# Second-layer rows of a two-layer mixture of experts: whole rows turned by TensorE, or quarter rows turned by VectorE in 32 by 32 squares

## The chip, the cores and the metric

One core of one Trainium2 chip runs the whole program. The metric is the device time of one execution in microseconds (us). Before the change it is 563.17 us, the median of three runs (561.17 to 566.2).

## What is computed

An attention without softmax, an RMS norm, and two layers of a mixture of experts with one expert per token. Cut to what matters here, the second layer:

```python
N, D, E, F = (2304, 512, 8, 1024)
expert_idx = np.argmax(x @ w_gate, axis=1)
gate_w = probs[np.arange(N), expert_idx]
...
disp[e, counts[e]] = x[i]          # rows sorted by expert
h = np.maximum(np.einsum('ecd,edf->ecf', disp, w1), 0.0)
y = np.einsum('ecf,efd->ecd', h, w2)
out[i] = gate_w[i] * y[expert_idx[i], pos[i]]
```

All tensors are float32. The first layer is the same, on the normed output of the attention.

## The kernel before

**Blocks.** Each layer is a list of blocks: a block holds up to 320 rows of one expert. The second layer has ten, counted from 0 here; their widths are 256, 256, 256, 268, 320, 260, 176, 160, 144 and 256 rows, for the experts in places 0, 0, 1, 1, 2, 3, 4, 5, 6 and 7 of an order by load. The function moe() runs them one after the other. Phase 1 of a block multiplies w1 with the block's rows (tiles hps on TensorE, eight steps `fc`), phase 2 multiplies w2 with what phase 1 gave (tiles acc, eight steps again). A product of two float32 numbers is made of three matmuls of rounded parts (h for high, l for low: lines 1275, 1276, 1277), and in blocks 6 to 8, under 192 rows wide ("plain"), of one float32 product (line 1273). The weights come as eight pieces per expert through SP's queue (raw, or w where a block is plain); ScalarE makes the high part of a piece (line 1169), VectorE the low part (line 1172).

**How rows reach a block.** The first layer stores its result by rows in DRAM (x2d). While block k runs, GpSimd gathers the rows of block k+1 into tiles xg of up to 128 rows: one indirect DMA per tile (line 1201), four xg buffers. A tile has rows on the partitions and 512 values along them; the matmuls want it turned, values on the partitions. x_tile() does that with four TensorE transposes of 128 by 128 into PSUM (xps, line 1251). ScalarE then writes the high part xh (line 1259) and VectorE the low part xl (line 1267). These steps are taken up one by one in phase 2 of block k, one after each `fc` from 1 on; every engine works its own instructions in program order. In the same steps an odd `fc` takes one piece of the next expert's w1 (ScalarE's high part, VectorE's low part), if block k+1 has another expert and is not plain. The first matmuls of block k+1 read xh, and the second one xl, over the whole width of the block.

**The first layer has both ways.** From its fourth block on its rows are gathered in quarters: gather_quarters() issues one indirect DMA for 32 rows, 128 partitions of 128 values each (line 1212), and x_squares() turns a tile with one VectorE instruction on 32 by 32 squares (xw, line 1226). ScalarE and VectorE then read xw where they would have read xps.

**What else is on the queues.** GpSimd also scatters the results: blocks 3 to 8 in quarters (line 1460, one indirect DMA per 32 rows, after a VectorE product with the gate, line 1456), the other blocks in tiles of 128 rows (line 1326). All indirect DMAs stand in one queue, in program order. final() works out the routing of the layer in small VectorE steps; rest() is its last part, and by_quarter() copies three kinds of numbers to the partitions of the quarters by four small matmuls.

```python
for k, b in enumerate(blocks):
    ...
    if k and nb and (m or "gi" in rt):
        nb.gather()
    ...
        slot(fc % 2, ahead, RATES[m][1] if nb else THEN2)
        ...
        if fc:
            run(xs, 1)
```

Here nb is the next block, xs the list of its turning steps, and slot() takes the pieces of weights, the scatters and the routing steps.

Of the kernel before, what the change touches and what calls it, by code (L numbers as in the profile page):

```python
# [11 lines left out]
F32 = mybir.dt.float32  # L12
# [11 lines left out]
N, DM, E, F = 2304, 512, 8, 1024  # L24
# [7 lines left out]
DC = DM // 128  # L32
# [33 lines left out]
OFF = (1152, 1536)  # L66
# [27 lines left out]
def plain(c):  # L94
    return slice(128 * c, 128 * c + 128)
# [6 lines left out]
def up(w):  # L102
    return (w + 31) // 32 * 32
# [75 lines left out]
class Kernel:  # L179
# [546 lines left out]
    def rest(self, m, rt, lo, hv, ncol, nt, c0, x=""):  # L726

        V = self.nc.vector
        A = [128, nt, ncol]
        k = 2 + m  # L730
        got = rt["got"]
        parts = rt["parts"] + ([self.tokw[:, 0:ncol]] if m else [])
        pv = self.rp.tile([128, k, nt, ncol], F16, tag="pv" + x, name="pv" + x)
        for i in range(k):
            V.tensor_tensor(out=pv[:, i], in0=hv[:, 0], in1=bc(parts[i], 1, A), op=ALU.mult)
            yield 0.4
        yield 2 * PE_WAIT
        ps = yield from self.picked(lo, pv, ncol, nt, k)
        val = self.t([128, 2, nt], F32, "G" + x)
        G = val[:, 0]  # L740
        V.tensor_copy(out=G, in_=ps[:, 0])
        V.scalar_tensor_tensor(out=G, in0=ps[:, 1], scalar=1 / 4096, in1=G, op0=ALU.mult, op1=ALU.add)
        if m:
            none = self.t([128, nt], F32, "none" + x)
            V.tensor_scalar(
                out=none, in0=got[:, 0], scalar1=-4096.0, scalar2=float(4096 + OFF[0]), op0=ALU.mult, op1=ALU.add
            )
            si = self.t([128, nt], I32, "si" + x)
            V.tensor_tensor(out=si, in0=ps[:, 2], in1=none, op=ALU.add)
            rt["si"] = si  # L750
            V.tensor_tensor(out=val[:, 1], in0=ps[:, 2], in1=none, op=ALU.add)
        elif c0 is not None:
            V.tensor_copy(out=self.aux[:, c0:c0 + nt, E], in_=got[:, 1])
            V.tensor_copy(out=self.aux[:, c0:c0 + nt, E + 1], in_=got[:, 0])
        self.hold = False
        rt["G"] = G
        yield
        if rt is self.rt[1]:
            yield 2 * PE_WAIT
            ps = yield from self.by_quarter(val.rearrange("p k n -> p (k n)"), 2 * nt)  # L760
            G4 = rt["G4"] = self.t([128, nt, 4], F32, "ex")
            V.tensor_copy(out=G4, in_=ps[:, :, 0:nt].rearrange("p g n -> p n g"))
            rt["si4"] = self.quarter_rows(ps[:, :, nt:], 0, "gi4")
            self.hold = False
            yield

# [451 lines left out]
    def x_squares(self, m, xg, n, xh, xl, o):  # L1218

        nc = self.nc  # L1220
        k = up(n) // 32
        src = xg[:, 0:k, 0:128].rearrange("p g (c d) -> p c g d", c=4)
        xw = self.mp.tile([128, DC, 128], F32, tag="xw", name="xw", bufs=2)

        def turn():
            nc.vector.transpose(out=xw[:, :, 0:32 * k].rearrange("p c (g t) -> p c g t", t=32), in_=src)  # L1226

        return [turn, lambda: self.x_parts(m, xw[:, :, 0:n], xh, xl, o, n)]
# [16 lines left out]
    def x_tile(self, m, x, n, xh, xl, o, ps=None):  # L1245

        if ps is None:
            ps = self.pt.tile([128, 512], F32, tag="t", name="xps")
        ps = ps.rearrange("p (a b) -> p a b", a=4)
        for dc in range(DC):  # L1250
            self.nc.tensor.transpose(  # L1251
                out=ps[:, dc, 0:n], in_=x[:n, plain(dc)], identity=self.c("ident")[:n, :n]
            )
        self.x_parts(m, ps[:, :, 0:n], xh, xl, o, n)

# [518 lines left out]
    def run(self):  # L1774
# [10 lines left out]
        ]  # L1785
        for b in self.blocks[0][SQUARES:]:
            b.squares = True
        for b in self.blocks[1]:
            b.turned = b.w % 128 > 0
        self.feed = [Feed(self, m) for m in range(2)]  # L1790
        self.rp = ctx.enter_context(tc.tile_pool(name="route", bufs=1))
        self.rawp = ctx.enter_context(tc.tile_pool(name="raw", bufs=4))
# [21 lines left out]
class Block:  # L1814
# [15 lines left out]
    def gather(self):  # L1830
        if self.xgs or self.xt or self.squares and "gi4" not in self.rt:
            return
        for t in range(tiles_of(self.w)):
            n = min(128, self.w - 128 * t)
            self.xgs.append((
                self.k.gather_quarters(self.m, self.t0 + t, n) if self.squares else
                self.k.gather(self.m, self.rt["gi"], self.t0 + t, n, self.known), n,
            ))
        if self.squares:
            for xg, n in self.xgs:  # L1840
                self.k.normal(xg[:, 0:up(n) // 32], 128, self.k.nc.gpsimd)

# [110 lines left out]
def pieces(name, a):  # L1953

    if name == "moe2_w2":
        a = a.reshape(E, F, 4, DC, 32).transpose(0, 1, 3, 2, 4).reshape(E, F, DM)
    if name.endswith("w1"):
        return a.reshape(E, DC, 128, 4, 256).transpose(0, 3, 2, 1, 4).reshape(E, 4, 128, 1024)
    return a.reshape(E, 4, 2, 128, DM).transpose(0, 1, 3, 2, 4).reshape(E, 4, 128, 1024)
# [43 lines left out]
```

## Time and profile before

| | |
|---|---|
| median of three runs | 563.17 us (561.17 to 566.2) |
| the profiled execution | 565.43 us, of it 563.6 us in the span of its instructions |
| TensorE busy | 97% of the span, 3980 matmuls |
| VectorE, ScalarE, GpSimd busy | 56%, 41%, 32% |
| granted TensorE clock, mean | 0.992 of full speed |

The profile is one execution on the chip. An instruction's row names the engine, the line, what it writes and reads, and its duration; starts are in us from the first instruction. Matmuls overlap, so that a matmul's own duration (0.28 us, say) is longer than the step from one start to the next. The second layer's blocks 2 to 9 lie between some 354 and 558 us.

### The profile page before, as it was taken

To read this page: it belongs to the slowest core of one execution; us is meant where nothing else is said; L and a number is where in the kernel's file an instruction comes from. 1 tells how busy PE (TensorE), PEld (TensorE's weight loads), DVE (VectorE), ACT (ScalarE), POOL (GpSimd) and SP (SyncE) were. 2 spreads that over 40 slices of the span, in tenths; PEclk is the share of its full clock that TensorE was granted. 3 is DMA by queue.
4 is the path that set the end of the run, shared out by engine and by line. 5 is a ranking of instruction groups with operands and counts; after the bars stand their busy time and mean duration, and the time that the engine had idled before them with its cause. 6 is when DMAs were issued, how large, how long until landed. Compare 5 with 4: busy or idle time off the path is not lost.

```text
span 563.6 us, 10439 instructions
## 1 busy us (share of the span) xinstructions
PE 544.5 (97%) x3980; PEld 516.2 (92%) x3980; DVE 316.5 (56%) x742; ACT 231.4 (41%) x414; POOL 178.3 (32%) x182
## 2 busy tenths in 40 slices
PE   7899999999999999999989999999999999999995
PEld 6889769999999999999978988989899999999994
DVE  1357962677666667767787695375146562221470
ACT  0255422344555555555553541255243532211440
POOL 1232313475526070812001001212312725643241
PEclk9999999999999999999998998999999999999999
DMA  8996935256555565665545514246234656889531
GB/s 307 389 371 232 393 91 189 95 181 218 179 167 175 178 197 182 205 199 180 188 155 185 176 45 150 75 149 211 74 99 158 204 190 199 273 248 333 197 110 41
DMA packets 34229, 106.93 MB, mean 190 GB/s; under 512 B 6664, under 2 KB 6794, under 8 KB 34171
## 3 DMA queue, kind: packets, MB, share of 16 engines
q1 hardware_dynamic: 24432, 81.95, 42.9%
q0 software_dynamic: 7072, 19.48, 11.1%
q10 hardware_dynamic: 2667, 4.75, 2.5%
q8 instruction: 33, 0.54, 0.4%
q14 instruction: 25, 0.20, 0.1%
HBM read 91.83 MB, written 14.60 MB: 189 GB/s over the span
## 4 chain that ended last, share of the span: by engine, by line
PE 73%; DVE 8%; DMA 7%; issue 5%; POOL 4%; ACT 2%; SPq 0%; POOLq 0%; ACTq 0%; DVEq 0%
PE hps L1275 8%; PE hps L1276 8%; PE hps L1277 8%; PE acc L1275 7%; PE acc L1277 7%; PE acc L1276 7%; PE hps L1273 7%; PE acc L1273 6%; PE yps L1405 3%; POOL xg L1212 3%; DMA qkv<-in_v_dram 2%; PE o L406 2%; PE kv L1273 2%; PE xps L1251 2%; DMA qkv<-in_k_dram 2%
## 5 line engine op out<-in xcount | busy, mean ns | idle before, releaser
L1275 PE MATMUL hps<-xh,w1h 128*128 128x256 f32 (+9 forms) x448 | 132.4, 296 | 0.0
L1276 PE MATMUL hps<-xl,w1h 128*128 128x256 f32 (+9 forms) x448 | 130.2, 291 | 1.0 <-DVE xl L1263 0.9
L1277 PE MATMUL hps<-xh,w1l 128*128 128x256 f32 (+9 forms) x448 | 129.7, 289 | 0.0
L1296 ACT ACTIVATE hh<-hps 128x256 fp32r<-128x256 f32 (+13 forms) x144 | 54.6, 379 | 149.7 <-PE hps L1277 99.7
L1275 PE MATMUL acc<-hh,w2h 128*128 128x320 f32 (+8 forms) x320 | 95.6, 299 | 0.0
L1277 PE MATMUL acc<-hh,w2l 128*128 128x320 f32 (+8 forms) x320 | 94.4, 295 | 0.0
L1276 PE MATMUL acc<-hl,w2h 128*128 128x320 f32 (+8 forms) x320 | 94.4, 295 | 0.0
L1276 PEld LDWEIGHTS hps<-xl,w1h 128*128 128x128 f32 x448 | 84.8, 189 | 1.9 <-DVE xl L1263 1.5
L1275 PEld LDWEIGHTS hps<-xh,w1h 128*128 128x128 f32 x448 | 84.8, 189 | 1.6 <-issue 1.5
L1277 PEld LDWEIGHTS hps<-xh,w1l 128*128 128x128 f32 x448 | 84.8, 189 | 0.0
L1298 DVE SCALAR_TENSOR_TENSOR hl<-hps,hh 128x256 fp32r<-128x256 f32 (+9 forms) x112 | 49.0, 439 | 53.6 <-ACT hh L1296 53.2
L1212 POOL DMA_INDIRECT xg<-x1d,gi x54 | 55.0, 1019 | 72.9 <-DVE xw L1226 58.9
L1460 POOL DMA_INDIRECT out_dram<-y,gi x44 | 49.7, 1131 | 67.7 <-DVE y L1456 51.4
L1172 DVE TENSOR_TENSOR w2l<-raw,w2h 128x1024 fp32r<-128x1024 f32 x48 | 58.6, 1222 | 20.3 <-ACT w2h L1169 20.3
L1172 DVE TENSOR_TENSOR w1l<-raw,w1h 128x1024 fp32r<-128x1024 f32 x48 | 58.8, 1242 | 14.2 <-ACT w1h L1169 13.5
L1275 PEld LDWEIGHTS acc<-hh,w2h 128*128 128x128 f32 x320 | 61.1, 191 | 0.3
L1276 PEld LDWEIGHTS acc<-hl,w2h 128*128 128x128 f32 x320 | 61.2, 191 | 0.0
L1277 PEld LDWEIGHTS acc<-hh,w2l 128*128 128x128 f32 x320 | 61.1, 191 | 0.0
L1169 ACT ACTIVATE w2h<-raw 128x1024 fp32r<-128x1024 f32 x48 | 50.5, 1054 | 5.6 <-ACT y L1409 5.6
L1169 ACT ACTIVATE w1h<-raw 128x1024 fp32r<-128x1024 f32 x48 | 49.2, 1048 | 0.0
L1273 PE MATMUL acc<-hh,w 128*128 128x224 f32 (+3 forms) x256 | 40.9, 314 | 0.0
L1273 PE MATMUL hps<-xh,w 128*128 128x224 f32 (+3 forms) x256 | 39.4, 313 | 0.1
(308 smaller groups left out, 778.0 us busy)
## 6 DMA issues: line engine op xcount, KB each, us to landing
raw<-in_moe_w_dram SPq DMA_DIRECT2D x96, 512.0 KB, 3.4
w<-in_moe_w_dram SPq DMA_DIRECT2D x32, 512.0 KB, 4.7
x1d<-xs POOLq DMA_DIRECT2D x4, 1056.0 KB, 6.4
qkv<-in_k_dram SPq DMA_DIRECT2D x8, 512.0 KB, 9.0
qkv<-in_v_dram SPq DMA_DIRECT2D x8, 512.0 KB, 8.5
qkv<-in_q_dram SPq DMA_DIRECT2D x8, 512.0 KB, 7.3
x2d<-y ACTq DMA_DIRECT2D x15, 256.0 KB, 2.5
xg<-x1d,gi POOLq DMA_INDIRECT x57, 2.9
```

The lines of the kernel that those rows point to most:

```text
L406: T.matmul(out=ps[:, pair, 0:144], lhsT=qt[b, i // 2][:, at:at + 128], rhs=kvs[b][:, pair], start=True, stop=True)
L1169: self.nc.scalar.activation(out=h, in_=t, func=ACTF.Copy)
L1172: (self.nc.gpsimd if eng == "P" else self.nc.vector).tensor_tensor(out=l, in0=t, in1=h, op=ALU.subtract)
L1212: self.nc.gpsimd.indirect_dma_start(out=xg[:, g], out_offset=None, in_=(self.X1, self.X2)[m].rearrange("n (q x) -> (n q) x", q=4), in_offs ...
L1273: nc.tensor.matmul(out=out, lhsT=a[0], rhs=b[0], start=start, stop=stop)
L1275: nc.tensor.matmul(out=out, lhsT=a[0], rhs=b[0], start=start, stop=False)
L1276: nc.tensor.matmul(out=out, lhsT=a[0], rhs=b[1], start=False, stop=False)
L1277: nc.tensor.matmul(out=out, lhsT=a[1], rhs=b[0], start=False, stop=stop)
L1296: nc.scalar.activation(out=hh[:, fc, :], in_=ps, func=ACTF.Relu)
L1298: nc.vector.scalar_tensor_tensor(out=hl[:, fc, :], in0=ps, scalar=0.0, in1=hh[:, fc, :], op0=ALU.max, op1=ALU.subtract)
L1405: nc.tensor.matmul(out=ps[:n, j, :], lhsT=yt[:, dc, 128 * t:128 * t + n], rhs=self.iwg[:, dc, :], start=True, stop=True)
L1460: self.nc.gpsimd.indirect_dma_start(out=out, out_offset=bass.IndirectOffsetOnAxis(ap=rt["si4"][:, g - g0, t0 + t:t0 + t + 1].bitcast(U32), ...
```

## The change

Blocks 3 to 9 of the second layer take the way of the first layer's later blocks: rows gathered in quarters, turned by one VectorE instruction per tile. In the first layer a square holds 32 neighbouring values of a quarter row. Here the values stand in another order: chunk c of the turned tile takes every fourth value, so that VectorE reads its input with a step of four values (16 bytes). The rows of w1 of the second layer are put in the same order ahead of the run, and so blocks 0 to 2, still turned by TensorE, read every fourth column too (`x[:n, dc::DC]` as the operand that is loaded as weights). rest() works out one more table, the gather indices of the quarters.

```diff
-        val = self.t([128, 2, nt], F32, "G" + x)
+        val = self.t([128, 2 + m, nt], F32, "G" + x)
...
             V.tensor_tensor(out=val[:, 1], in0=ps[:, 2], in1=none, op=ALU.add)
+            V.tensor_copy(out=val[:, 2], in_=got[:, 1])
...
-            ps = yield from self.by_quarter(val.rearrange("p k n -> p (k n)"), 2 * nt)
+            ps = yield from self.by_quarter(val.rearrange("p k n -> p (k n)"), 3 * nt)
...
-            rt["si4"] = self.quarter_rows(ps[:, :, nt:], 0, "gi4")
+            rt["si4"] = self.quarter_rows(ps[:, :, nt:2 * nt], 0, "gi4")
+            rt["gi4"] = self.quarter_rows(ps[:, :, 2 * nt:], OFF[1], "gj4")
...
-        src = xg[:, 0:k, 0:128].rearrange("p g (c d) -> p c g d", c=4)
+        src = xg[:, 0:k, 0:128].rearrange("p g (d c) -> p c g d" if m else "p g (c d) -> p c g d", c=DC)
...
-                out=ps[:, dc, 0:n], in_=x[:n, plain(dc)], identity=self.c("ident")[:n, :n]
+                out=ps[:, dc, 0:n], in_=x[:n, dc::DC] if m else x[:n, plain(dc)], identity=self.c("ident")[:n, :n]
...
-        for b in self.blocks[1]:
+        for i, b in enumerate(self.blocks[1]):
             b.turned = b.w % 128 > 0
+            b.squares = i > 2
...
-        if self.squares:
+        if self.squares and self.m == 0:
...
+    if name == "moe2_w1":
+        a = a.reshape(E, 128, DC, F).transpose(0, 2, 1, 3).reshape(E, DM, F)
```

What moves on the engines, at the three places that are spoken of later. In the rows below, line numbers of the changed kernel are two higher (1172 is 1174, 1201 is 1203, 1212 is 1214, 1226 is 1228, 1251 is 1253, 1267 is 1269, 1273 is 1275, 1460 is 1462).

First, GpSimd's queue from the gather for block 5 to the end of the second layer, before (y_ and a number are the results of blocks 4 to 8):

```order
L1201 DMA xg<-x2d,gi 128x512
L1201 DMA xg<-x2d,gi 48x512
L1460 DMA out_dram<-y_5382,gi_4233 9216x128 x10
L1201 DMA xg<-x2d,gi 128x512
L1201 DMA xg<-x2d,gi 32x512
L1460 DMA out_dram<-y_5695,gi_4233 9216x128 x9
L1201 DMA xg<-x2d,gi 128x512
L1201 DMA xg<-x2d,gi 16x512
L1460 DMA out_dram<-y_5862,gi_4233 9216x128 x6
L1201 DMA xg<-x2d,gi 128x512 x2
L1460 DMA out_dram<-y_6019,gi_4233 9216x128 x5
```

The same stretch after (gj is the new table of indices):

```order
L1214 DMA xg<-x2d,gj_4239 128x128 x6
L1462 DMA out_dram<-y_5380,gi_4235 9216x128 x10
L1214 DMA xg<-x2d,gj_4239 128x128 x5
L1462 DMA out_dram<-y_5691,gi_4235 9216x128 x9
L1214 DMA xg<-x2d,gj_4239 128x128 x5
L1462 DMA out_dram<-y_5855,gi_4235 9216x128 x6
L1214 DMA xg<-x2d,gj_4239 128x128 x8
L1462 DMA out_dram<-y_6009,gi_4235 9216x128 x5
```

The places are the same; where two gathers stood there are five to eight.

Second, VectorE in phase 2 of block 8, where block 9 is prepared (w1l is the low part of a piece of w1), before:

```order
L1172 TENSOR_TENSOR w1l<-raw,w1h 128x1024
L1267 TENSOR_TENSOR xl<-xps,xh 128x4x128 x2
L1172 TENSOR_TENSOR w1l<-raw,w1h 128x1024 x3
L1449 MEMSET acc 128x16
L1450 STREAM_TRANSPOSE y_6194<-acc 128x5x32
```

And after:

```order
L1174 TENSOR_TENSOR w1l<-raw,w1h 128x1024
L1228 STREAM_TRANSPOSE xw<-xg 128x512
L1269 TENSOR_TENSOR xl<-xw,xh 128x4x128
L1174 TENSOR_TENSOR w1l<-raw,w1h 128x1024
L1228 STREAM_TRANSPOSE xw<-xg 128x512
L1269 TENSOR_TENSOR xl<-xw,xh 128x4x128
L1174 TENSOR_TENSOR w1l<-raw,w1h 128x1024 x2
L1451 MEMSET acc 128x16
L1452 STREAM_TRANSPOSE y_6184<-acc 128x5x32
```

The second tile's xl stood behind one piece of w1; now it stands behind two pieces and two turns.

Third, TensorE in the same phase, before (hh and w are the operands of phase 2):

```order
L1273 MATMUL hps<-xh,w 128x144 x32
L1273 MATMUL acc<-hh,w 128x144 x8
L1251 MATMUL xps<-ct,xg 128x128 x4
L1273 MATMUL acc<-hh,w 128x144 x4
L1251 MATMUL xps<-ct,xg 128x128 x4
L1273 MATMUL acc<-hh,w 128x144 x20
```

And after, with the first products of block 9 behind it:

```order
L1275 MATMUL hps<-xh,w 128x144 x32
L1275 MATMUL acc<-hh,w 128x144 x32
L1277 MATMUL hps<-xh,w1h 128x256
L1278 MATMUL hps<-xl,w1h 128x256
L1279 MATMUL hps<-xh,w1l 128x256
```

The eight transposes are gone, and the 32 products of phase 2 stand in one row ahead of the first ones of block 9.

## Rows read from the trace of the kernel before

**Rows 1.** Busy time of each engine by stretch; PEclk is the granted clock.

```profile
core 0: us, PE busy (x) PEld busy (x) DVE busy (x) ACT busy (x) POOL busy (x), PEclk, DMA share, GB/s
340.00:360.00 20.00, 19.27 (x119) 17.09 (x119) 7.58 (x24) 4.17 (x9) 5.87 (x6) 0.91 0.38 135
356.00:546.00 190.00, 190.00 (x1406) 184.46 (x1405) 86.77 (x172) 68.38 (x126) 71.72 (x68) 1.00 0.57 186
```

**Rows 2.** Timeline of TensorE: start, duration, then the instruction, at phase boundaries.

```profile
401.89 0.28 PE L1275 MATMUL hps<-xh,w1h 128*128 128x268 f32 x1
...
413.41 0.28 PE L1275 MATMUL acc<-hh,w2h 128*128 128x268 f32 x1
...
416.30 0.60 PE L1251 MATMUL xps<-ct,xg 128*128 128x128 f32 x4
416.65 0.37 PE L1275 MATMUL acc<-hh,w2h 128*128 128x268 f32 x1
...
426.70 0.31 PE L1275 MATMUL hps<-xh,w1h 128*128 128x320 f32 x1
...
440.78 0.31 PE L1275 MATMUL acc<-hh,w2h 128*128 128x320 f32 x1
...
518.52 0.29 PE L1273 MATMUL hps<-xh,w 128*128 128x144 f32 x1
...
526.36 0.29 PE L1273 MATMUL acc<-hh,w 128*128 128x144 f32 x1
...
534.99 0.38 PE L1275 MATMUL hps<-xh,w1h 128*128 128x256 f32 x1
```

**Rows 3.** Instructions on tile xw (first layer) and xps: ns min/median/max.

```profile
L1226 DVE STREAM_TRANSPOSE xw<-xg x17: 297/703/705, 133.3 to 282.8; 128x512 f32<-128x512 f32 x11, 128x128 f32<-128x128 f32 x3, 128x256 f32<-128x256 f32 x2, 128x384 f32<-128x384 f32 x1
L1259 ACT ACTIVATE xh<-xw,g x17: 322/723/725, 134.0 to 283.4; 128x512 fp32r<-128x512 f32 x11, 128x224 fp32r<-128x224 f32 x1, 128x176 fp32r<-128x176 f32 x1, 128x80 fp32r<-128x80 f32 x1
...
L1267 DVE TENSOR_TENSOR xl<-xps,xh x17: 168/691/693, 312.9 to 531.0; 128x512 fp32r<-128x512 f32 x14, 128x48 fp32r<-128x48 f32 x1, 128x256 fp32r<-128x256 f32 x1, 128x16 fp32r<-128x16 f32 x1
```

**Rows 4.** Operations with and without a step in their input: by line, ns.

```profile
L1029 DVE TENSOR_TENSOR pf<-pf,oh x2: 425/462/499, 77.9 to 329.5; 128x144 f32<-128x144 f32 x1, 128x184 f32<-128x184 f32 x1
L619 DVE TENSOR_TENSOR pf<-sp,run x3: 307/309/351, 77.6 to 329.1; 128x144 f32<-128x144 f32 x2, 128x184 f32<-128x184 f32 x1
L610 PE MATMUL sp<-oh,triw x2: 417/450/483, 76.4 to 326.9; 128*128 128x144 f16 x1, 128*128 128x184 f16 x1
...
L332 PE MATMUL sp<-warm x62: 269/273/421, 1.0 to 82.2; 128*128 128x256 f16 x62
L661 PEld LDWEIGHTS <-lo 128*128 128x128 f16 x82 | 7.8, 144 | 1.3 <-issue 1.0 <-DVE hl L1298 0.3
L1251 PEld LDWEIGHTS xps<-ct,xg 128*128 128x128 f32 x68 | 8.4, 145 | 1.0 <-PE sp L661 0.3
```

**Rows 5.** Timeline of GpSimd at its indirect DMAs, and the gathers' time to landing.

```profile
381.07 0.99 POOL L1201 DMA_INDIRECT xg<-x2d,gi  x1 [0.30 <-PE hps L1277]
382.36 0.97 POOL L1201 DMA_INDIRECT xg<-x2d,gi  x1 [0.30 <-issue]
...
461.03 1.76 POOL L1460 DMA_INDIRECT out_dram<-y,gi  x1 [11.49 <-DVE y L1456]
...
478.34 0.99 POOL L1201 DMA_INDIRECT xg<-x2d,gi  x1 [0.31 <-issue]
...
510.52 0.98 POOL L1201 DMA_INDIRECT xg<-x2d,gi  x1 [0.30 <-issue]
...
xg<-x2d,gi POOLq DMA_INDIRECT x21, 3.8
```

**Rows 6.** Timelines of ScalarE and VectorE at the start of phase 2 of blocks 3 and 8.

```profile
413.90 1.05 ACT L1169 ACTIVATE w1h<-raw 128x1024 fp32r<-128x1024 f32 x1
...
526.75 1.05 ACT L1169 ACTIVATE w1h<-raw 128x1024 fp32r<-128x1024 f32 x1
...
527.83 1.22 DVE L1172 TENSOR_TENSOR w1l<-raw,w1h 128x1024 fp32r<-128x1024 f32 x1 [7.83 <-ACT w1h L1169]
```

## The prediction

> **What bounds the kernel now.** Busy time by stretch comes first. [...] The timeline of TensorE, the second view, tells what a transpose takes of it; the timelines of the others tell whether they follow. The profiled execution took 565.43 us, 2.26 above the median; the sum is made against it and 2.26 taken off at the end.
>
> **What is removed.** 17 tiles of blocks 3 to 9, four transposes each. One group starts at 416.30, the next product at 416.65; the pipeline loses more around it, so I compare whole phases. Block 3's two phases have the same 96 matmuls: phase 1 runs from 401.89 to 413.41, 11.52 us, phase 2 with three tiles from 413.41 to 426.70, 13.29: 1.77, or 0.59 a tile. Block 8: 518.52 to 526.36 is 7.84, 526.36 to 534.99 with two tiles 8.63: 0.79, or 0.40 a tile [rows 2]. Seventeen tiles lie between 6.8 and 10.0 us; between two ends that near, the middle: **8.4 us gained**.
>
> **TensorE's own new price.** Blocks 0 to 2 keep TensorE, 6 tiles, 24 transposes, and now load weights with a step of 16 bytes. No row shows a float32 load with a step. Upper bound: the small products of the routing read their moving operand with exactly that step (16 bytes), and 184 columns took 483 ns where 144 took 417, so 1.65 ns per column, while 256 columns without a step took 269 ns in all [rows 4]. 128 columns would take 211 ns, where a transpose now passes in about 0.35/4 = 0.09 to 0.11; 0.11 more each, 0.45 a tile, 2.7 for six. One of the six, near 347 us, lies in a stretch with a mean clock of 0.91 [rows 1], where the products are slow already, so 2.2. Lower bound: loads of 16-bit columns with a step (lo) take 144 ns, those of float32 without one 145 [rows 4]: nothing lost. I take **2.2 us**, since the moving operand's row has the same step.
>
> The trace shows a stepped read four times as dear on TensorE's moving side, and not on its weight side, for 16-bit data. [...]
>
> **VectorE's new price.** A turn of a full tile took 703 ns in the first layer, where it reads 32 neighbours in a row [rows 3]. Here each value is 16 bytes from the last. Nearest row: a product of 144 values one of whose inputs has a step of 16 bytes takes 425 ns, one of the same size without a step 307; 0.82 ns more per value [rows 4]. For 512 values 0.42 us: a turn of 1.12 us. Bounds: 0.70, if a turn is free of it, and 1.24, if each value took as long again as in the first layer (703 ns for 512 values, 297 for 128: 1.06 ns each). 12 us more on VectorE are in nobody's way as a sum; what counts is the chain in phase 2 of the block before.
>
> [...]
>
> **Who is late next.** In phase 2 the pieces of w1 and the tiles take turns: high part of a piece on ScalarE (1.05), its low part on VectorE (1.2) [rows 6], turn (1.12), xh on ScalarE (0.72, with its start 0.75) [rows 3], and only then the next piece's high part, because ScalarE works in order. A round is 4.1 us. Before, the transposes were TensorE's and the rounds ran beside each other.
> - Block 8: ScalarE starts 0.4 us into the phase (526.75 against 526.36). Two rounds end at 8.6, the last xl (0.69) at 9.3. Phase 2 without transposes is 7.84 long [rows 2]. Block 9's second product waits **1.5 us**. With a turn of 0.70 it would be 0.6.
> - Block 3: start 0.5 us in (413.90 against 413.41), two rounds to 8.7, a third piece 2.25, and the half tile of block 4 (64 rows) at about half a round's turn, xh and xl, 1.3: 12.3. The phase without transposes is 11.52: **0.8 us**. With 0.70, none.
> - Block 4 has 14.08 us for its phase (426.70 to 440.78 is the same number of products) and a last tile of 4 rows: three pieces, two full tiles and a small one fit, with some 1.5 to spare. In blocks 2, 5, 6 and 7 no weights are split in phase 2 (the same expert follows, or a plain one), and the turns have the phase to themselves.
> So 2.3 us at two places, bounds 0.6 and 2.8 (turn of 0.70 and of 1.24).
>
> **GpSimd's queue.** 52 gathers in place of 17: 35 more, 1.29 us from one to the next (381.07 to 382.36) [rows 5], 45 us on an engine with 118 us idle in the stretch. What is late at the worst place? The scatters of block 4 start at 461.03 and now end before 478.34. From there: 5 gathers, 9 scatters, 5 gathers, 6 scatters, 8 gathers, 33 times 1.29 = 42.6, end 520.9; now the last two gathers start at 510.52. They land 3.8 us after issue [rows 5], at 523.4 for the last. Block 9's second turn would be asked for some 6.7 us into block 8's phase 2, at 533 in today's time, and the scatters of block 4 move ahead with TensorE. Cover of 9 us before the saving of the blocks between (under 4): no cost. If that cover is gone, each us late costs one.
>
> **Routing.** Three more VectorE operations on at most 84 values a partition, each under the 0.31 us of 144 values [rows 4]. Only the copy into val stands ahead of TensorE's quarter products. 0.2 us, bounds 0 and 0.9.
>
> **Sum.** -8.4 + 2.2 + 2.3 + 0.2 = -3.7: 561.7 for an execution like the profiled one, and **559.5 us** against the median, 0.7% faster.
>
> **Rivals.**
> - *No price for the step at all.* For it: the first layer's turn, the weight loads of lo. Against it: two engines show one. -8.4 + 0.6 + 0.2 = -7.6: 555.6. The same with TensorE alone spared: -5.9, 557.3.
> [...]
> - *The turn is dearer than any row here shows, and every block start waits; slower.* Each 0.1 us more per turn costs 0.25 at block 4 and 0.2 at block 9; from a turn of about 1.9 us on the gain is gone. At 2.6 the two places cost 6.7 more, and block 5 (the 1.5 us that were to spare go in 2.5 tiles times 1.5 us more) and block 3 some 2 each: -3.7 + 6.7 + 4.0 = +7.0, 570.2. For it: the price of the step on a four-deep pattern is not in the trace.
> - *GpSimd's gathers come late.* The queue of 33 has no gap from 478 on, and VectorE then stands still at a turn with everything behind it, the pieces of weights and the freeing of acc too. At 3 us late twice: +6 - 3.7 = +2.3, 565.5. Against it: the 9 us above.
>
> **How the numbers follow.** 45% for the forecast, with its own range of 558 to 561.5; 10% for no price at all and 17% for VectorE's alone; 13% for the clock; 7% for the dear turn; 8% for late gathers. A measurement of this kernel tells about 1% from no change, that is 557.5 and 568.8. Under 557.5 lie the case of no price, half of VectorE's alone and a little of the forecast: 0.25. Over 568.8 half of the dear turn: 0.04. Within: 0.71. The range leaves out the case of no price in its lower half and the upper rivals: 555.5 to 563.6.
>
> **What the next profile would show.** 24 transposes at line 1253 in place of 92, their step from start to start near 0.2 us (or still 0.11). Turns in the second layer of 1.1 us for 512 values (or 0.7). Waits of TensorE for VectorE's xl at the first products of blocks 4 and 9 of about 1 and 1.5 us, none at blocks 3, 5, 6, 7 and 8. Phase 2 of block 8 at 7.84 us. The prediction fails if TensorE waits at other places, if turns wait for gathers that have not landed, or if the phases do not shrink to the length of those without transposes.

## The result, and the profile after

The changed kernel took 558.0 us (median of 7 runs, 556.19 to 559.39) where the kernel before, run beside it, took 565.14 (561.17 to 566.2): a ratio of 0.9878 with a 95% interval of 0.9849 to 0.9908, 1.2% faster. Forecast were 559.5 us in a range of 555.5 to 563.6. That is the first group of runs. Four more groups followed, each on one chip with its own runs of the kernel before, and in two of these it was slower than the kernel before: 598 us in one, and 602 for a variant of it in the other. That is told with the experiments.

The execution that was profiled took 556.19 us, its span is 554.4, its mean granted clock 0.998 (before: 565.43, 563.6 and 0.992). The 9.2 us between the two lie in two places. The stretch from block 1's phase 1 to block 9's phase 2 is the one that the change can reach. First the kernel before, then the changed one, busy time by stretch as in [rows 1]:

```profile
354.56:546.60 192.04, 192.04 (x1422) 186.50 (x1421) 86.96 (x172) 69.26 (x128) 72.98 (x69) 1.00 0.56 184
```

```profile
core 0: us, PE busy (x) PEld busy (x) DVE busy (x) ACT busy (x) POOL busy (x), PEclk, DMA share, GB/s
351.49:537.49 186.00, 185.19 (x1353) 180.67 (x1352) 100.39 (x189) 69.35 (x128) 107.77 (x103) 1.00 0.57 191
```

It shrank by 6.04 us, from 192.04 to 186.00, at a granted clock of 1.00 both times: that is the change's own gain, where 3.7 were forecast. TensorE is no longer busy for all of it (185.19 of 186.00), VectorE does 13.4 us more and GpSimd 34.8. The other 3.1 us were gained ahead of the stretch, and they are not the change's: the profiled execution of before had half the clock for 3.4 us twice (0.50 from 305.8 to 309.2 and from 346.8 to 350.2), where the profiled one after has 1.00 from 300 to 550. The mean clock varies from one execution to the next with either kernel: 0.991 to 0.998 in the seven of the changed one, 0.992 to 0.999 in the seven of the kernel before that ran beside the longer pause below.

TensorE's timeline at the boundaries of the blocks, the counterpart of [rows 2]: start, duration, instruction, and in brackets the idle time ahead of it and what ended it.

```profile
409.30 0.28 PE L1277 MATMUL acc<-hh,w2h 128*128 128x268 f32 x1
...
421.23 0.31 PE L1277 MATMUL hps<-xh,w1h 128*128 128x320 f32 x1
421.38 0.40 PE L1278 MATMUL hps<-xl,w1h 128*128 128x320 f32 x1
421.62 0.30 PE L1279 MATMUL hps<-xh,w1l 128*128 128x320 f32 x1
...
516.57 8.00 PE L1275 MATMUL acc<-hh,w 128*128 128x144 f32 x64
524.89 0.38 PE L1277 MATMUL hps<-xh,w1h 128*128 128x256 f32 x1 [0.31 <-ACT xh L1261]
525.62 0.38 PE L1278 MATMUL hps<-xl,w1h 128*128 128x256 f32 x1 [0.34 <-DVE xl L1269]
...
528.79 0.36 PE L1277 MATMUL hps<-xh,w1h 128*128 128x256 f32 x1 [0.16 <-DVE acc L1451]
```

Block 3's phase 2 runs from 409.30 to 421.23, 11.93 us where it was 13.29. Block 4 starts with next to no wait: its second product, which needs xl, comes 0.15 us after the first, and the third 0.24 after that, 0.1 more than usual. Block 9 waits three times: for xh, for xl, and some 3 us later for a part of acc that VectorE clears (L1451; the product of 528.79 starts 0.44 us after the one ahead of it, where 0.12 is usual). Its phase 1 is 12.60 us long (524.89 to 537.49) where it was 11.61, and block 8's phase 2 is 8.32 (516.57 to 524.89) where the same number of products takes 7.84 in its phase 1: 1.47 us for the start of block 9. (Phase 2 without a wait turns out to take 7.75, in the order experiment below; against that it is 1.56.)

The tiles, as in [rows 3]; the first line holds both layers, its maximum is the second's:

```profile
L1228 DVE STREAM_TRANSPOSE xw<-xg x34: 298/705/1130, 132.9 to 523.1; 128x512 f32<-128x512 f32 x22, 128x128 f32<-128x128 f32 x7, 128x256 f32<-128x256 f32 x4, 128x384 f32<-128x384 f32 x1
L1261 ACT ACTIVATE xh<-xw x17: 216/629/633, 390.3 to 524.2; 128x512 fp32r<-128x512 f32 x8, 128x512 f32<-128x512 f32 x3, 128x48 fp32r<-128x48 f32 x1, 128x256 fp32r<-128x256 f32 x1
...
  DMA xg<-x2d,gj: 2.7, 3
```

VectorE's turn of 512 values takes 1.10 us (its single instructions stand in the next fence), xh 0.63. Three turns waited for a gather, 2.7 us together, without a wait of TensorE behind them. The weight load with a step, and a group of four transposes with the product behind it, as in [rows 2, 4]:

```profile
L1253 PEld LDWEIGHTS xps<-ct,xg x24: 195/208/218, 309.8 to 367.9; 128*128 128x128 f32 x24
```

```profile
365.76 0.64 PE L1253 MATMUL xps<-ct,xg 128*128 128x128 f32 x4
366.15 0.47 PE L1277 MATMUL acc<-w2h,hh 128*128 128x512 f32 x1
```

The load grew from 145 to 208 ns, but the group passes in 0.39 us where it took 0.35.

Block 8's phase 2 on VectorE and ScalarE, the counterpart of [rows 6]:

```profile
518.04 1.23 DVE L1174 TENSOR_TENSOR w1l<-raw,w1h 128x1024 fp32r<-128x1024 f32 x1 [7.83 <-ACT w1h L1171]
519.19 1.10 DVE L1228 STREAM_TRANSPOSE xw<-xg 128x512 f32<-128x512 f32 x1
520.98 0.69 DVE L1269 TENSOR_TENSOR xl<-xw,xh 128x512 fp32r<-128x512 f32 x1 [0.70 <-ACT xh L1261]
521.93 1.22 DVE L1174 TENSOR_TENSOR w1l<-raw,w1h 128x1024 fp32r<-128x1024 f32 x1 [0.25 <-ACT w1h L1171]
```

```profile
516.96 1.05 ACT L1171 ACTIVATE w1h<-raw 128x1024 fp32r<-128x1024 f32 x1
520.32 0.63 ACT L1261 ACTIVATE xh<-xw 128x512 fp32r<-128x512 f32 x1 [2.31 <-DVE xw L1228]
520.86 1.04 ACT L1171 ACTIVATE w1h<-raw 128x1024 fp32r<-128x1024 f32 x1
```

This is the round of the forecast, one engine at a time: w1h, w1l, turn, xh, and the next w1h only 3.90 us after the first (516.96 to 520.86).

### The profile page after: what moved, and what is told of

Read it like the earlier page. It is cut to its first block, busy times and chain, and to the rows that moved or that the text cites. A ratio compares the mean times of both kernels' runs of the same rounds, so it can differ in the third digit from the quotient of the medians.

```text
span 554.4 us, 10373 instructions
## 1 busy us (share of the span) xinstructions
PE 534.9 (96%) x3912; PEld 507.9 (92%) x3912; DVE 331.1 (60%) x763; ACT 231.6 (42%) x414; POOL 212.3 (38%) x217
## 4 chain that ended last, share of the span: by engine, by line
PE 34%; issue 22%; DMA 17%; POOL 13%; DVE 10%; ACT 3%; POOLq 1%; SPq 0%; ACTq 0%; DVEq 0%
POOL xg L1214 9%; DMA xg<-x1d,gi 6%; DMA out_dram<-y,gi 4%; PE hps L1278 4%; PE hps L1279 4%; PE hps L1277 4%; PE acc L1277 3%; PE acc L1279 3%; PE acc L1278 3%; DMA qkv<-in_v_dram 2%; PE hps L1275 2%; PE o L406 2%; POOL out_dram L1462 2%; DVE w1l L1174 2%; PE kv L1275 2%
## 5 line engine op out<-in xcount | busy, mean ns | idle before, releaser
L1277 PE MATMUL acc<-hh,w2h 128*128 128x320 f32 (+8 forms) x320 | 94.3, 295 | 0.0
L1214 POOL DMA_INDIRECT xg<-x2d,gj x52 | 51.6, 993 | 15.8 <-issue 13.4
L1275 PE MATMUL acc<-hh,w 128*128 128x224 f32 (+3 forms) x256 | 39.7, 313 | 0.0
```

The lines of the kernel that those rows point to most:

```text
L1214: self.nc.gpsimd.indirect_dma_start(out=xg[:, g], out_offset=None, in_=(self.X1, self.X2)[m].rearrange("n (q x) -> (n q) x", q=4), in_offs ...
L1275: nc.tensor.matmul(out=out, lhsT=a[0], rhs=b[0], start=start, stop=stop)
L1277: nc.tensor.matmul(out=out, lhsT=a[0], rhs=b[0], start=start, stop=False)
```

## The experiments

**What the step costs VectorE, and what block 9 waits for.** The squares read 32 neighbours in a row, as in the first layer, and the six tiles that stay with TensorE are sorted by GpSimd ahead of their transposes.

```diff
-        src = xg[:, 0:k, 0:128].rearrange("p g (d c) -> p c g d" if m else "p g (c d) -> p c g d", c=DC)
+        src = xg[:, 0:k, 0:128].rearrange("p g (c d) -> p c g d", c=DC)
...
-        a = a.reshape(E, 128, DC, F).transpose(0, 2, 1, 3).reshape(E, DM, F)
+        a = a.reshape(E, 4, DC, 32, F).transpose(0, 2, 1, 3, 4).reshape(E, DM, F)
...
+            steps.insert(max(0, len(steps) - 1), lambda xg=xg, n=n, x=x: k.sorted(m, xg, n, k.nc.gpsimd, x))
```

> The squares read 32 neighbours in a row (the rows of moe2_w1 sorted to match), and the six tiles that TensorE turns are sorted by GpSimd first, so that nothing has a step of 16 bytes. If the step sets the price of a turn and the turn is what block 9 waits for: turns of 0.70 us for 512 values where the changed kernel has 1.10, block 9's wait 1.35 -> 0.3 to 0.6 us, TensorE's stepped weight loads back at 140 ns, and the stretch from block 1's phase 1 to the end about 1.1 us shorter: 557. If block 9 waits for the pieces of weights or for the gathers: the turn gets shorter and the wait stays over 1.2 us, time as the changed kernel's. If the sorting by GpSimd is late: new waits at blocks 0 to 2 of up to 1 us each.

558.35 us, ratio to before 0.9874 (0.9834 to 0.9914). Turns, and the start of block 9:

```profile
L1228 DVE STREAM_TRANSPOSE xw<-xg x34: 297/704/712, 133.2 to 525.2; 128x512 f32<-128x512 f32 x22, 128x128 f32<-128x128 f32 x7, 128x256 f32<-128x256 f32 x4, 128x384 f32<-128x384 f32 x1
```

```profile
526.86 0.38 PE L1284 MATMUL hps<-xh,w1h 128*128 128x256 f32 x1
527.36 0.39 PE L1285 MATMUL hps<-xl,w1h 128*128 128x256 f32 x1
```

No turn takes over 0.712 us any more: the step of 16 bytes is the whole difference to 1.10. That is 0.78 ns a value. Block 9's phase 1 falls from 12.60 to 12.38 us and block 8's phase 2 from 8.32 to 7.75: 0.79 less together, so 0.4 us of turn give 0.79 at block 9, the 0.2 for 0.1 of the forecast's two rounds. What this saves is lost again at block 1, whose second tile waits for GpSimd's sorting (0.9 us, and 0.7 in phase 1): the stretch is 185.77 long.

**What the step costs TensorE.** The kernel before, with the new order of w1's rows and `x[:n, dc::DC]` for all 23 tiles; nothing else of the change.

```diff
-                out=ps[:, dc, 0:n], in_=x[:n, plain(dc)], identity=self.c("ident")[:n, :n]
+                out=ps[:, dc, 0:n], in_=x[:n, dc::DC] if m else x[:n, plain(dc)], identity=self.c("ident")[:n, :n]
```

> The kernel before, with the rows of moe2_w1 in the new order and all 23 tiles of the second layer turned by TensorE through a step of 16 bytes: the step on TensorE alone. By the forecast's price (0.11 us for each of 92 transposes): +10 us, ratio 1.018. By what the changed kernel's trace shows (weight loads 145 -> 208 ns, but a group of four from 0.35 to 0.39 us, the loads beside the matmul ahead): 23 times 0.04, +1.0 us, ratio 1.002, no difference that can be measured.

566.08 us against 565.36, ratio 1.0008 (0.9979 to 1.0036): no difference that can be measured, where the forecast's price would be 10 us. The loads:

```profile
L1251 PEld LDWEIGHTS xps<-ct,xg x92: 190/210/221, 311.5 to 530.6; 128*128 128x128 f32 x68, 12*128 12x128 f32 x4, 64*128 64x128 f32 x4, 4*128 4x128 f32 x4
```

In the profile the stretch is 193.96 us long where it was 192.04: 1.92 for the 19 tiles in it, 0.10 each (forecast: 0.45). A full tile pays 0.04; the last tiles of blocks, of 4 to 64 rows, pay some 0.2 (0.37 to 0.61 for the 48 rows of block 6). The loads of small tiles are about as long as those of full ones (190 to 221 ns over all 92). My reading, which no run here separates: a load is hidden by the transpose ahead of it as far as that one lasts, and a transpose passes as many columns as the tile has rows.

**The order in phase 2.** The steps of the next block's tiles are written ahead of the piece of weights, two at a time.

```diff
             for fc in range(FC):
+                if m and nb and nb.squares:
+                    run(xs, 2)
                 if rows:
```

> In phase 2 of the second layer the turn and its parts are written ahead of the piece of weights, two steps at a time, where the next block has squares. If block 9 waits because a turn stands behind the high part of a weight in the round: its wait of 1.35 us at the first products goes, the last piece of w1 comes at about the same time as before, and the time falls by 1.3 us to 556.7. If the sum of the work in the phase is what counts: the wait moves to the third or fourth piece of w1 in block 9's phase 1, and the time stays. If the gathers have not landed by then, VectorE stands still at the turn with the weights behind it: slower by 1 to 3 us.

556.4 us, ratio 0.9852 (0.981 to 0.9895), the fastest of all. The stretch, then VectorE and ScalarE in block 8's phase 2:

```profile
351.65:535.99 184.34, 184.34 (x1354) 180.48 (x1352) 100.54 (x189) 69.26 (x128) 111.32 (x104) 1.00 0.59 193
```

```profile
520.09 0.69 DVE L1269 TENSOR_TENSOR xl<-xw,xh 128x512 fp32r<-128x512 f32 x1 [0.69 <-ACT xh L1261]
521.04 4.63 DVE L1174 TENSOR_TENSOR w1l<-raw,w1h 128x1024 fp32r<-128x1024 f32 x4 [0.26 <-ACT w1h L1171]
```

Both tiles are ready at 520.8, four pieces of weights follow one another, and block 9 starts at 524.39 without a wait. TensorE is busy for all of the 184.34 us; against the changed kernel's 186.00 that is 1.66, of it 1.56 at the start of block 9 (phase 2 of block 8 takes 7.75 here, phase 1 of block 9 takes 11.60) and 0.09 at block 4. So the order is what block 9 waited for: the same turns of 1.10 us cost nothing once they stand ahead. The timed runs cannot tell this kernel from the changed one (556.4 and 558.0, their ranges overlap); in the profile the difference is plain.

**Both together.** The edits of the first and the third experiment.

> Neighbours in a row and the turn ahead of the weights, together. If both theories hold they do not add at block 9, whose 1.35 us can go only once: about 1.5 us off the changed kernel (1.35, 0.1 at block 4, 0.25 of TensorE's loads, less what the sorting costs), 556.5, and no wait of TensorE over 0.3 us at the start of any block from 3 on. If the gathers bound the turns: no better than with the order alone.

557.74 us, ratio 0.9861 (0.9821 to 0.9902). No wait at block 9 and none at block 4, but block 1's for the sorting stays: the stretch is 184.99. The shorter turn is worth nothing once the order is right.

**Three that met something else.** The next four ran beside one another, with the kernel before at 567.17 us. In the first, every turn of the second layer is made twice; in the second, each quarter gather is issued twice; in the third, squares stand from block 6 on only (`b.squares = i > 5`); the fourth is the changed kernel again.

> The changed kernel with every turn of the second layer made twice: 17 times 1.1 us more on VectorE, some 18 us. By the chain of the forecast (a turn holds up the next piece of weights): 2.2 more at block 9, 2.75 at block 4 less the 0.7 by which the changed kernel was earlier there than forecast, 1.2 at block 5 (2.75 less 1.5 that were to spare): 5.5 us, 563.5. By the slope that the squares of 32 neighbours showed at block 9 (0.57 for 0.40, so 1.6 for 1.1) and nothing elsewhere: 559.5. If VectorE is in nobody's way: 558.

> The changed kernel with each quarter gather of the second layer issued twice: 52 more at 1.26 us, 65 us more on GpSimd, which stood idle for some 73 us between 381 and 510 less what the first 35 took. If GpSimd's queue still has the cover of 9 us that the forecast gave it: the queue of about 33 instructions from block 4's scatters on grows by 18, 23 us, less 9 of cover: TensorE waits 14 us in all at the starts of blocks 7 to 9, 572. If the waits hit every block from 5 on: up to 20 us, 578. If the cover is far larger than I counted: 558.

> The changed kernel with squares for blocks 6 to 9 alone: 8 of the 17 tiles, the other 9 turned by TensorE with its step of 16 bytes. If the gain is that of the tiles (8.0 us for 17 in the profile, 0.47 each, and 0.10 more for each that TensorE turns with a step): 9 times 0.57, 5.1 us slower than the changed kernel, 563.1, with block 9's wait unchanged. If the gain comes from the head of the program (the two stretches at half clock that the profile of before had and that of the changed kernel had not): near 558.

> The changed kernel once more, beside the others of this call, for the clock in its head. If the two stretches at half clock that its profile lacked are a matter of chance: some executions have them, and the profiled one shows them or not with the rest of the timeline the same; the product of span and mean granted clock stays near 553. If the change itself removed them: none has them, and the clock stays at 0.998.

Measured: 605.79, 704.76, 586.68, and for the unaltered changed kernel 598.17, a ratio of 1.0562 (1.0508 to 1.0616) where the first group gave 0.9878. So first the fourth. Up to 376 us its timeline is that of the first group. Then, for the stretch and for a part of block 3:

```profile
352.10:574.96 222.86, 199.13 (x1353) 190.06 (x1352) 99.81 (x189) 68.92 (x128) 107.59 (x103) 0.94 0.47 160
...
405.00:429.00 24.00, 16.44 (x109) 15.37 (x108) 3.12 (x8) 4.08 (x11) 15.33 (x16) 0.81 0.19 61
```

222.86 us where the first group had 186.00, with the same instructions and the same busy time on VectorE, ScalarE and GpSimd. What TensorE's weight loads do in block 2's phase 1:

```profile
384.77 0.19 PEld L1277 LDWEIGHTS hps<-xh,w1h 128*128 128x128 f32 x1
384.89 0.19 PEld L1278 LDWEIGHTS hps<-xl,w1h 128*128 128x128 f32 x1
385.97 0.19 PEld L1279 LDWEIGHTS hps<-xh,w1l 128*128 128x128 f32 x1 [0.89 <-issue]
386.08 0.19 PEld L1277 LDWEIGHTS hps<-xh,w1h 128*128 128x128 f32 x1
386.70 0.19 PEld L1278 LDWEIGHTS hps<-xl,w1h 128*128 128x128 f32 x1 [0.43 <-issue]
387.41 0.19 PEld L1279 LDWEIGHTS hps<-xh,w1l 128*128 128x128 f32 x1 [0.52 <-issue]
```

Until 385 a load starts every 0.12 us. From there on they come in clumps whose first ones start some 0.7 us apart or a multiple of it (385.97, 386.70, 387.41), in the middle of an accumulation, where no semaphore is waited for ("issue"). Each such time begins inside a row of indirect DMAs on GpSimd, one every 1.26 us, at the eighth to eleventh of the row, and ends some 1 to 3 us after its last: here a row from 376.0 to 390.5 and clumps from 385.0 to 392.3; then 405.4 to 425.3 and 416.0 to 428; then rows that end at 495.7, 519.1 and 543.2, with clumps from 490.8 and 514.3 and a stop from 539.9. One row of the same trace goes nearly free: fifteen DMAs from 447.0 to 469.4, nine scatters ahead of six gathers, with a single gap of 0.70 us behind them. In the stretches with the longer clumps the mean granted clock is lower, 0.88 from 375.5 to 405 and 0.81 from 405 to 429; from 441 to 538, with the clumps from 490.8 and 514.3 in it, it is 1.00. In the groups without clumps the rows were as long: in the order experiment 46 indirect DMAs follow one another from 456.4 to 516.7 beside a TensorE that is never idle.

Ahead of the clumps something else goes wrong: TensorE's work is reported late. Each of the eight steps of block 2's phase 1 ends with a product that ScalarE waits for. Such a product of TensorE (the one of the fourth step), then ScalarE ("remote" stands for a semaphore update whose sender the profile does not show):

```profile
381.17 0.28 PE L1279 MATMUL hps<-xh,w1l 128*128 128x256 f32 x1
```

```profile
380.25 0.39 ACT L1298 ACTIVATE hh<-hps 128x256 fp32r<-128x256 f32 x1 [0.32 <-PE hps L1279]
384.58 0.39 ACT L1298 ACTIVATE hh<-hps 128x256 fp32r<-128x256 f32 x1 [3.94 <-PE hps L1279]
384.86 1.05 ACT L1171 ACTIVATE w2h<-raw 128x1024 fp32r<-128x1024 f32 x1
390.29 0.39 ACT L1298 ACTIVATE hh<-hps 128x256 fp32r<-128x256 f32 x1 [4.38 <-remote]
```

In the first group ScalarE follows each of the eight products 0.32 us after its start. Here it follows by 0.32, 0.32, 0.53, 3.42, 7.68, 7.75, 5.51 and 1.21 us: late from the row's fourth DMA on, and by 3.42 us for the product of 381.17, while TensorE still starts a product every 0.12 us. Only as the lateness grows further does TensorE stop. The stop from 539.9 to 545.5 is of the same kind: sixteen products have started by 539.94, ScalarE follows the first eight at 545.35, and seven updates of TensorE's semaphore come in a bunch from 545.01 to 545.36. So the clumps are not shown to be a lack of instructions; whether TensorE finishes late or only its updates are late, the trace does not tell.

The traces of the two groups with clumps differ in one more thing. Of some 1500 semaphore updates that the engines' instructions send, 110 to 165 have no record in each of the seven traces of these groups, that of the kernel with next to no clumps (plain gathers, below) among them; in the seven others none is missing. So the recording did not go as in the other groups either. Every timed execution here has a recorded span and clock, and no run tells whether the clumps would be there without the recorder.

Read with that in mind, the other three still tell something. *Turns made twice*, block 8's phase 2, VectorE and then ScalarE:

```profile
565.68 1.23 DVE L1174 TENSOR_TENSOR w1l<-raw,w1h 128x1024 fp32r<-128x1024 f32 x1 [8.17 <-ACT w1h L1171]
566.83 2.23 DVE L1229 STREAM_TRANSPOSE xw<-xg 128x512 f32<-128x512 f32 x2
```

```profile
564.60 1.05 ACT L1171 ACTIVATE w1h<-raw 128x1024 fp32r<-128x1024 f32 x1
569.10 0.63 ACT L1262 ACTIVATE xh<-xw 128x512 fp32r<-128x512 f32 x1 [3.44 <-DVE xw L1229]
569.63 1.04 ACT L1171 ACTIVATE w1h<-raw 128x1024 fp32r<-128x1024 f32 x1
```

The round is 5.03 us long (564.60 to 569.63), 1.13 more than 3.90; block 8's phase 2 is 10.54 and not 8.32. So 1.1 us of turn give 2.2 at block 9, the forecast's 0.2 for 0.1. The total of 605.79 beside 598.17 is not read, since clumps lie in both.

*Squares from block 6 on.* Before its first clump, block 1's phase 1 to the end of block 5's takes 114.35 us (354.17 to 468.52); in the changed kernel of the first group 109.37 (351.49 to 460.86). The nine tiles that are back with TensorE cost 4.98 us, 0.55 each; expected were 5.1.

*Gathers issued twice.* The second of a pair writes where the first did, and the profile shows GpSimd waiting for a gather to land ahead of the next one, so the gathers come in twos some 4 us apart, and far more is added than the 65 us of the expectation: turns wait 171 us for gathers, TensorE 128 us for xh. It is worth something for another reason: it has twice the quarter gathers, in rows of two or three, and TensorE's clumps are gone from all of these; the only two clumps between 370 and 545, at 520.2 and 521.6, stand at the end of a row of eleven. Two later rows of twelve and eleven (548.7 to 564.3 and 587.0 to 601.3, ten and nine of them scatters) have none. So the number of gathers alone does not bring the clumps. Whether it is the length of the row or the pace, which was about half of the usual one here, is not separated, and TensorE stood waiting for xh much of the time.

**Rows of gathers taken away, or broken.** The order experiment once more, and two kernels made from it beside it (before: 570.91 us). In the first, each tile is gathered in one piece of whole rows, in the second a memset on GpSimd follows each quarter gather.

```diff
+        if m:
+            return self.gather(m, self.rt[m]["gi"], t, 128).rearrange("p (g x) -> p g x", g=4)
```

```diff
+            if m:
+                self.nc.gpsimd.memset(self.mp.tile([128, 128], F32, tag="pause", name="pause", bufs=1), 0.0)
```

> The squares ahead of the weights once more, in another call, because the call before this one gave 598 us for the changed kernel where the earlier calls gave 558: there TensorE's matmuls came in clumps 0.70 us apart, without a semaphore that they waited for, from the eighth to eleventh of an unbroken row of indirect DMAs on GpSimd until two or three us after the row's end. If that belongs to the chip or to its state in that call, this run gives 556 to 557, or some 596 with the same clumps on a chip like it. If it belongs to the one kernel as it was loaded there, 556 to 557 on any chip.

> The squares ahead of the weights, but each tile is gathered in one piece of 128 whole rows, 17 gathers in place of 52; the squares then turn the quarters of wrong rows, so the values of blocks 3 to 9 are not the reference's, and everything else is done as before. If the 35 more gathers cost nothing on a chip without the clumps (the forecast's cover): as the kernel beside it, 556 to 557, within 1 us. If they cost something through the queue: up to 2 us less. On a chip with the clumps: if the rows of gathers bring them, they are gone or nearly so, 556 to 560 against 596.

> The squares ahead of the weights, with a memset of 128 by 128 on GpSimd behind each quarter gather of the second layer, so that none directly follows another: 52 pauses of about 0.5 us and 0.3 to start, 25 to 40 us more on GpSimd. If GpSimd has the cover of 9 us at its worst place and 73 us in the stretch: no wait of TensorE over 1 us, 556 to 559. If the queue from block 4's scatters on is the limit (23 quarter gathers there, 0.8 each, 18 us less 9 of cover): turns of blocks 7 to 9 wait for gathers, 9 us, 566. On a chip with the clumps: if unbroken rows of indirect DMAs are what brings them, they are gone and the time is as on the other; if the number of gathers is, they stay, near 596.

602.37 us, a ratio of 1.058 (1.0514 to 1.0645), for the very kernel that was the fastest before; 561.72, a ratio of 0.9861 (0.9803 to 0.9918), with plain gathers; 594.22 with the memset. The stretch with plain gathers:

```profile
352.55:538.42 185.87, 185.26 (x1354) 180.60 (x1352) 99.64 (x189) 68.72 (x128) 73.53 (x69) 1.00 0.59 197
```

With everything but the 35 additional gathers the stretch is 185.87 us long, where the kernel beside it took 226.97: the 41 us between them go with the quarter gathers and their long rows. Most of what is left over 184.34 stands right behind two rows of seven (0.84 and 0.45 us in blocks 6 and 7). A tile then holds whole rows where the squares expect quarters, so blocks 3 to 9 get other values than the reference; the instructions behind the gathers are the same. The memset took only 0.22 us, and most gathers still came 1.33 us apart. The first row, of two scatters and nine gathers, lost its clumps by it, the later ones of 11 to 16 did not. So a row need not be unbroken to bring clumps. With plain gathers ScalarE still follows TensorE late in block 2's phase 1, beside a row of five, but by no more than 2.17 us: the row ends before the lateness has grown. In the groups without clumps it is 0.32 at these eight products in every kernel.

**A longer pause.** The order experiment with a product of 128 by 512 on GpSimd ahead of every second quarter gather (before: 562.62).

```diff
+            if m and g % 2 == 0:
+                i = bc(self.c("ident"), 1, [128, DC, 128])
+                p = self.mp.tile([128, DC, 128], F32, tag="pause", name="pause", bufs=1)
+                self.nc.gpsimd.tensor_tensor(out=p, in0=i, in1=i, op=ALU.mult)
```

> The squares ahead of the weights, with a product of 128 by 512 on GpSimd (about 1.04 us) ahead of every second quarter gather of the second layer, so that gathers come at the first layer's pace: at most about five in 10 us where they were eight. On a chip with the clumps: if an unbroken row of eight or more indirect DMAs is what brings them, they stay only where nine scatters stand in a row ahead of gathers (before blocks 7 to 9), the blocks 2 to 4 are free of them, and the time falls from some 600 to 575 to 585; if their number in the stretch is, nothing changes. On a chip without: GpSimd has 28 times 1.3, 36 us more; with the forecast's cover of 9 us at the worst place no wait before block 7 and up to 6 us of waits of turns for gathers from there: 557 to 563; with no cover left, 570.

574.53 us, ratio 1.0217 (1.0179 to 1.0255). The longest waits of VectorE and of TensorE:

```profile
DVE xw L1232 <- DMA xg<-x2d,gj: 46.4, 8, 12.4
```

```profile
PE hps L1281 <- ACT w1h L1171: 7.2, 1, 7.2
PE hps L1279 <- ACT xh L1265: 2.2, 1, 2.2
PE hps L1281 <- ACT xh L1265: 1.4, 1, 1.4
```

There is no clump, but there is none either in its rows of eight and ten scatters, the kernel before was at its lowest of all groups, and no semaphore update is missing in this trace: this group was probably free of them anyway, so the run does not tell whether such pauses help. Its chip has the number 1, like that of the group before. If the number means the same piece, that piece had the clumps seven minutes earlier, and they belong to a state and not to the chip; whether it does is not known. What the run does tell is the price of late gathers: with 31 us more of busy time on GpSimd, turns waited 46.4 us for gathers and TensorE 12.7 us, at the starts of blocks 3, 4, 8 and 9 above all.

## Why the prediction was right, and where it was not

Its steps against the profile of the first group, in the stretch of 192.04 us.

- **The transposes taken from TensorE.** 8.4 us forecast. TensorE was busy for all of the 192.04 us before, at a granted clock of 1.00, so that what was taken from it there could be gained whole. The seven phases of blocks 2 to 8 lost 1.51, 1.36, 1.40, 1.01, 0.99, 0.98 and 0.79 us, 8.04 in all, once the wait at the end of the last is left out. The upper end of 0.59 a tile was read against block 3's phase 1; against its own phase 2 without tiles it is 0.45 (13.29 less 11.93, for three tiles). Shown a second time by the nine tiles put back.
- **TensorE's step: the term that was wrong.** 2.2 us forecast for 24 transposes, 0.11 each. The load did grow as estimated (208 ns, where the moving operand of the routing gave 211), but the step that failed is "0.11 more each". The loads run beside the products: in the group of 365.76 each load but the first starts as the transpose ahead of it does, and the transposes are 0.11 to 0.12 us apart, so that a full tile costs 0.04 us more in all. Six tiles cost about 0.25 us; the kernel with that step alone and 23 tiles was not measurably slower. The four times on the moving side stand on 1.65 ns a column against 0.43 (256 columns of the products on warm, one every 0.109 us). On the weight side a load with a step took 208 ns in float32 and 144 in 16 bits (lo); why they differ is not shown.
- **VectorE's step.** 1.12 us a turn forecast, 1.10 measured. The nearest row, a product with one input of that step, was the right one to take, and without the step the turn is 0.70.
- **Who is late next.** Block 9: 1.5 us forecast, 1.47 measured, by the chain that was named, and gone when its order is changed; about 0.3 us of it (the cleared acc) was not in the chain. Block 4: 0.8 forecast, 0.1 measured. The rounds are 3.9 us and not 4.1, since xh keeps ScalarE for 0.54 (520.32 to 520.86) where the forecast took 0.75 from the first layer's row (that one multiplies by g as well), and the phase that has to hide them is 11.93 long: I took block 3's phase 1 for it, 11.52.
- **GpSimd.** No cost forecast, and none found where there are no clumps, though three turns came to wait for gathers. The paused kernel shows that the margin is thin.
- **The clock.** 13% of the chances went to a lower clock. No run shows that waits at the starts of blocks bring it down: around those of block 9, from 516 to 530 us, it was 1.00.
- **Routing.** 0.2 us forecast, next to nothing found: TensorE's one wait there is 0.70 us (0.68 before), and the eight small products take 1.00 us (0.98 before).

The sum again with what was measured: -8.04 + 0.05 for the two stepped tiles of block 2 + 1.47 + 0.08 + 0.42 for block 3's phase 1 (below) = -6.02, and the stretch shrank by 6.04. The forecast was 2.3 us too cautious, 1.9 of it TensorE's step and 0.7 block 4's start. That the time lies within 1.5 us of the forecast all the same has a second reason: it started from 563.17, the median of three runs of before, where that of seven is 565.14. The gain was underestimated by 3.4 us (7.1 between the two medians of seven), the starting point by 2.0.

The forecast says nothing of the clumps, and in two groups of five they made the kernel, or its variant with the other order, 6% slower than before. Its rival of late gathers had the right engine and the wrong victim: there VectorE waits for a gather, here TensorE's updates come late, and then TensorE stops, while GpSimd issues. Shown is that in these two groups the clumps go when the quarter gathers go (plain gathers: none to speak of), that twice the gathers in twos some 4 us apart do not bring them, and that the same rows are harmless in other groups. Open is what in a chip, its state or the recording makes the difference, whether length or pace of a row counts, what GpSimd's issuing and TensorE have in common, and whether pauses cure it at a price below the gain. The kernel before may have some of it too: it took 567 and 571 us in these two groups and 563 to 565 in the others, and no trace of it from there was kept.

## What to carry to other kernels

Price a weight load by the step from one matmul to the next, not by its own duration: here 63 ns more in the load were 10 in the step. When work moves to another engine, look at the order in which it stands there before shortening it: here two lines of order gave all that a faster turn could. And a plan that fills a queue with one DMA after another wants to be timed in more than one group of runs before it is trusted: the same kernel was 7 us faster than the one before in one group, and 31 us slower in another.

## What the runs showed that was not expected

- TensorE's instructions in clumps some 0.7 us apart, mostly from the eighth to eleventh of a row of indirect DMAs on GpSimd, with its semaphore updates late, in two groups of five. Among the DMA packets the profile has a queue of the kind "instruction" (q8, 33 packets, 0.54 MB). One of its packets lies between 378 and 396 us and 13 between 350 and 590, in the first group and in the group with clumps alike. In the first group TensorE is busy without a gap at that packet (386.5 us). What these packets have to do with the clumps is not shown.
- Block 3's phase 1, 96 products of 268 columns, takes 11.94 us in the changed kernel and in its variants without clumps there, also in the one in which TensorE turns its tiles, and 11.52 in the kernel before and in the one with the step alone. No run here tells why.
